# Float32 weights kept in DRAM, low parts moved to VectorE, and steps placed elsewhere in the order of an attention, spectral mixing and FFN kernel

## The chip, the cores and the metric

The kernel runs on one core of a Trainium2 chip. The metric is device time in microseconds; the numbers compared are medians of runs. A core has five engines, each with its own in-order queue: TensorE (PE, with its weight loads as PEld), VectorE (DVE), ScalarE (ACT), GpSimd (POOL) and SyncE (SP), which here issues all transfers between DRAM and the on-chip memory. Matrix products land in PSUM, from which VectorE or ScalarE must take them.

## The reference

```python
# q, k, v: (8, 12, 448, 64); w_ch1: (768, 3072); w_ch2: (3072, 768); float32
scores = scale * np.matmul(q, k.transpose(0, 1, 3, 2)) - np.log(S)
attn = 1.0 / (1.0 + np.exp(-scores))
x = np.matmul(attn, v)             # heads side by side: (8, 448, 768)
mixed = np.real(fft(fft(x, axis=1), axis=2))
u = x + mixed
un = (u - mean(u)) / sqrt(var(u) + 1e-06)
out = u + np.maximum(un @ w_ch1, 0.0) @ w_ch2
```

## The kernel before

The 8 x 448 = 3584 tokens go through three stages.

**Attention and mixing** (the first 445 us or so, with a remainder up to about 485). Scores, sigmoid, values and the two Fourier transforms as products with cosine and sine tables; u is written to DRAM (`u_dram`). The largest weight is looked for here too, because the weights are scaled by a power of two (`wsc`).

**Two plain chunks** of 512 tokens each, numbers c = 0 and 1; the text calls them the first and the second chunk. A loop over f = 0..23 takes one 128-wide slice of the hidden layer at a time. TensorE does `up_proj(c, f)` (18 products into `psh`) and then `down_proj(c, f-1)` (24 products into `po`). `evac(c, f)` lies between: ScalarE writes the high half of the relu'd values, `hh` (float16), and VectorE the low half, `hl` = relu - hh. Each product of float32 numbers is made from three float16 products (high*high, high*low, low*high), and so the weights need high and low parts too.

In the first chunk the weights are made while they are used. There are 48 slices (24 of w1, 24 of w2; the list `order`), about two slots per iteration f, and a slot is `prep_step(k, 0..3)`, which calls `prep_w` for the slice at place k and for its neighbours: step 0 issues the load of slice k+2 and finishes slice k-1 (n == 4), step 1 is ScalarE's absolute value of slice k+1 (L381), steps 2 and 3 are VectorE's four instructions that turn slice k's float64 bits into a float32 number, `t` (tile `wt`; L383, L385, L389, L391). n == 4 scales `t` (L397, ScalarE), writes the high part `h` (L398, ScalarE) and the low part `l` = t - h (L399, GpSimd). An iteration in the engines' queues is: slot A, `evac`, slot B.

In the second chunk the parts are there already. Beside its products, `combine(i, p, n)` makes the sums of weight blocks that the fast chunks need, for 24 pairs of slices: n = 0 rebuilds float32 from h + l (tile `raw`), n = 1 makes four block sums (`cb`), n = 2 their high parts on ScalarE (`ch`), n = 3 their low parts on VectorE (`cl`), n = 4 writes them to `w_dram`. `made_at` says at which f. `fast_norm` (steps placed by `norm_at`) normalises and transposes the tokens of the first fast chunk: load of U, statistics, reciprocal root (`rsqrt`), scaling (L322, VectorE), transposes of 128 x 128 blocks on TensorE (`pst`, L674), copies, differences, and high and low parts (`ut`).

**Five fast chunks** of 512 tokens. Two 2 x 2 block products are each done with seven block products instead of eight (`UP_PRODUCTS`, `DOWN_PRODUCTS`: number of the product, index of the weight block, index of the token or value block). The order is a list of units: `fast_up` (9 products into one PSUM tile `psf`) or `fast_down` (6 products into `pso`), about 1 us each, 28 units per group g (7 up, 7 down, 7 up, 7 down), 6 groups per chunk, so 168 units per chunk. `later(d, fn)` puts a step d units further on in all queues. ScalarE and VectorE take each unit's PSUM tile (8 tiles, `ps_r`); relu, sums and the high and low parts of the hidden values (`F`, `H`) follow over the next units. `fast_norm` of the next chunk's two token halves (tp = 0, 1) is placed by the `later(t + ...)` lines, t being the chunk's first unit. A chunk's last products fall into the first 28 units of the chunk behind it; `fast_finish` then adds up the seven accumulators (`add`, L843), adds the residual (`put`, L847) and writes the output.

After every unit and iteration, `pin()` chains the instructions of each engine in the order in which the code made them, so that each queue runs in the order of the code.

## Time and profile before

| what | value |
|---|---|
| median of 3 runs | 1811.41 us (1811.26 to 1812.59) |
| the profiled execution's own time | 1814.86 us |
| its span, first to last instruction | 1813.1 us |
| PE busy | 1674.0 us (92%) |
| DVE busy | 1332.5 us (73%) |
| ACT busy | 640.3 us (35%) |
| POOL busy | 278.6 us (15%), none of it after about 671 us |
| mean granted TensorE clock | 0.972 |

Busy shares are means over stages with different limits; rows of one stage tell more. A wait is put down to whatever released it last. A granted clock of 1 is 2.4 GHz and of 0.5 is 1.2 GHz. Line numbers are those of the kernel before; the changed kernel's are one to five higher.

### The profile page before, as it was taken

To read this page: it belongs to the slowest core of one execution; us is meant where nothing else is said; L and a number is where in the kernel's file an instruction comes from. 1 tells how busy PE (TensorE), PEld (TensorE's weight loads), DVE (VectorE), ACT (ScalarE), POOL (GpSimd) and SP (SyncE) were. 2 spreads that over 40 slices of the span, in tenths; PEclk is the share of its full clock that TensorE was granted. 3 is DMA by queue.
4 is the path that set the end of the run, shared out by engine and by line. 5 is a ranking of instruction groups with operands and counts; after the bars stand their busy time and mean duration, and the time that the engine had idled before them with its cause. 6 is when DMAs were issued, how large, how long until landed. Compare 5 with 4: busy or idle time off the path is not lost.

```text
span 1813.1 us, 27651 instructions
## 1 busy us (share of the span) xinstructions
PE 1674.0 (92%) x10996; PEld 1070.8 (59%) x10996; DVE 1332.5 (73%) x2481; ACT 640.3 (35%) x815; POOL 278.6 (15%) x268
## 2 busy tenths in 40 slices
PE   8999999988888889897969998999899989999997
PEld 4555555544544445444547775777577757777774
DVE  3445576657999976788756878687868787877667
ACT  4434444435565641222214321422233223323221
POOL 4534444335334430000000000000000000000000
PEclk9999999999999999898989999999899999999999
DMA  7666767664555534444683654656465646565561
GB/s 230 212 211 198 240 206 229 203 194 118 190 162 170 173 124 148 148 168 170 217 312 143 231 221 165 241 220 229 166 231 211 236 177 233 193 233 230 218 229 55
DMA packets 98772, 357.21 MB, mean 197 GB/s; under 512 B 22369, under 2 KB 48210, under 8 KB 83154
## 3 DMA queue, kind: packets, MB, share of 16 engines
q1 hardware_dynamic: 98642, 355.44, 55.7%
q8 instruction: 86, 1.41, 0.3%
q14 instruction: 44, 0.36, 0.1%
HBM read 297.20 MB, written 55.05 MB: 194 GB/s over the span
## 4 chain that ended last, share of the span: by engine, by line
PE 37%; DVE 10%; ACT 2%; issue 1%; ACTq 0%; DVEq 0%
PE psf L769 18%; PE pso L820 18%; DVE F L775 2%; DVE acc L843 2%; DVE H L775 1%; ACT H L804 1%; DVE acc L829 1%; DVE ur L847 1%; PE pst L674 1%; ACT F L794 1%; DVE X L775 1%; DVE stt L295 1%; DVE U L322 0%; DVE mv L316 0%; DVE mv L315 0%
## 5 line engine op out<-in xcount | busy, mean ns | idle before, releaser
L769 PE MATMUL psf<-ut,ws 128*128 128x256 f16 x3780 | 426.7, 273 | 10.9 <-DVE ur L573 9.1
L820 PE MATMUL pso<-ws,H 128*128 128x384 f16 x2520 | 428.1, 329 | 3.3 <-ACT H L804 2.3
L769 PEld LDWEIGHTS <-ws 128*128 128x128 f16 x3780 | 371.0, 98 | 63.0 <-issue 12.4
L820 PEld LDWEIGHTS <-H 128*128 128x128 f16 x2520 | 248.5, 99 | 163.0 <-issue 6.5
L135 ACT ACTIVATE a<-sc 112x900 f32<-112x900 f32 x192 | 166.7, 918 | 163.8 <-PE sc L131 163.8
L829 DVE TENSOR_TENSOR acc<-pso,acc 128x384 f32<-128x384 f32 x350 | 181.2, 550 | 23.3 <-PE pso L820 23.3
L794 ACT ACTIVATE F<-F 128x1024 f32<-128x1024 f32 x60 | 63.5, 1058 | 381.1 <-DVE F L775 374.2
L151 PE MATMUL av<-a,vr 112*64 112x450 f32 x768 | 172.5, 572 | 3.7 <-DVE xT L160 3.7
L775 DVE TENSOR_TENSOR H<-F,H 128x1024 f16<-128x1024 f32 x120 | 129.5, 1088 | 55.8 <-ACT H L804 55.8
L552 PE MATMUL po<-w2h,hl 128*128 128x512 f16 (+1 forms) x384 | 129.0, 336 | 23.1 <-DVE hl L541 22.9
L533 PE MATMUL psh<-ut,w1h 128*128 128x512 f16 x504 | 149.9, 379 | 0.0
L775 DVE TENSOR_TENSOR F<-X,psf 128x256 f32<-128x256 f32 x240 | 98.9, 418 | 69.2 <-PE psf L769 67.1
L552 PE MATMUL po<-w2h,hh 128*128 128x512 f16 (+1 forms) x384 | 129.2, 337 | 8.1 <-ACT hh L540 7.3
L804 ACT ACTIVATE H<-F 128x1792 f16<-128x1792 f32 x60 | 101.8, 1697 | 88.1 <-DVE F L775 86.4
L160 DVE TENSOR_SCALAR xT<-av 128x450 f32<-128x450 f32 x48 | 30.1, 627 | 136.2 <-PE av L151 136.1
L552 PE MATMUL po<-w2l,hh 128*128 128x512 f16 (+1 forms) x384 | 128.9, 336 | 0.0
L552 PEld LDWEIGHTS <-hh 128*128 128x128 f16 x768 | 75.5, 101 | 62.7 <-ACT hh L540 17.2
L775 DVE TENSOR_TENSOR F<-F 128x256 f32<-128x256 f32 x240 | 91.2, 421 | 18.0 <-ACT F L794 13.2
L391 DVE SCALAR_TENSOR_TENSOR wt<-wr,wt 128x768 int32<-128x768 int32 x48 | 100.4, 2091 | 1.7
L151 PEld LDWEIGHTS av<-a,vr 112*64 112x64 f32 x768 | 48.0, 140 | 83.6 <-issue 68.8
L533 PE MATMUL psh<-ut,w1l 128*128 128x512 f16 x252 | 95.5, 379 | 0.0
L775 DVE TENSOR_TENSOR X<-X,psf 128x256 f32<-128x256 f32 x180 | 74.7, 415 | 28.1 <-PE psf L769 23.0
(95 smaller groups left out, 2066.4 us busy)
## 6 DMA issues: line engine op xcount, KB each, us to landing
ws<-w_dram SPq DMA_DIRECT2D x120, 1344.0 KB, 6.0
wr<-w_in SPq DMA_DIRECT2D x96, 768.0 KB, 4.5
qr<-q_in SPq DMA_DIRECT2D x48, 225.0 KB, 3.3
kr<-k_in SPq DMA_DIRECT2D x48, 224.0 KB, 3.5
vr<-v_in SPq DMA_DIRECT2D x24, 448.0 KB, 3.8
w_dram<-ch SPq DMA_DIRECT2D x24, 384.0 KB, 2.3
w_dram<-cl SPq DMA_DIRECT2D x24, 384.0 KB, 2.4
u_dram<-u SPq DMA_DIRECT2D x24, 336.0 KB, 4.1
```

The source lines that it names most:

```text
L135: nc.scalar.activation(a, ps[:CP, :, :SQ], AF.Sigmoid, bias=-math.log(S), scale=1.0 / math.sqrt(D))
L151: nc.tensor.matmul(ps[j * D:(j + 1) * D, :SQ], vr[:, c, h * D:(h + 1) * D], a[:, j], start=(c == 0), stop=(c == 3))
L391: nc.vector.scalar_tensor_tensor(out=ti, in0=hi, scalar=-0x40000000, in1=ti, op0=ALU.bitwise_and, op1=ALU.bitwise_or)
L533: nc.tensor.matmul(hs[c, f], l[f][:, m], r[:, m], start=(m == n == 0), stop=(m == NCC - 1 and n == 2))
L552: nc.tensor.matmul(po[n][:, at:at + hi - lo], l[:, cols], r[f][:, lo:hi], start=(f == 0 and m == 0 and at == 0), stop=(f == NFC - 1 and m ...
L769: nc.tensor.matmul(ps[:, :TH], w[:, x, a, m * 128:(m + 1) * 128], ut[y][:, b, m], start=(m == n == 0), stop=(m == n == 2))
L775: nc.vector.tensor_tensor(out=o, in0=x, in1=y, op=op)
L794: nc.scalar.activation(F[:, 0:4], F[:, 0:4], AF.Relu)
L804: nc.scalar.activation(hts[P][:, 0], F[:, 1:8], AF.Copy)
L820: nc.tensor.matmul(ps[:, :384], H[:, x, a, tp * 128:(tp + 1) * 128], w[:, y, b], start=(j == n == 0), stop=(j == 1 and n == 2))
L829: later(0, lambda: nc.vector.tensor_tensor(out=to, in0=ps[:, :384], in1=to, op=ALU.add))
L843: nc.vector.tensor_tensor(out=a[:, o], in0=a[:, o], in1=a[:, x], op=ALU.add)
```

## The change

- `prep_w`: one ScalarE instruction less per slice: the high part is made straight from `t` with the scale as operand, and now at n == 3, so at the end of the slice's own slot. The unscaled float32 `t` is written to a new DRAM tensor `t_dram` (384 KB per slice). The low part is made on VectorE, as t * scale - h, where n == 4 stood.
- `combine`: n = 0 is now a load from `t_dram` (768 KB), one iteration earlier, in place of two VectorE additions. The four sums are made in place, in other block orders, and scale is applied in n = 2 and n = 3.
- `made_at` and `norm_at`: pairs are spread otherwise over f (two at once at f = 9 and 16 instead of f = 1 and 12), and the transposes stand one f further behind the scaling.
- In the fast chunks `fast_norm` starts at unit 40 instead of 8 for the first half and at 98 instead of 88 for the second, and its transposes stand 8 units behind the scaling instead of 2. Both product tables have other orders, and `fast_finish` is called for every product of the last group, with each sum right behind the product that completes it, instead of all eleven steps behind the seventh.

```diff
@@ -45,8 +45,8 @@
 NPLAIN = 2
 NP = NFC // 2
 
-UP_PRODUCTS = ((1, 1, 1), (6, 4, 4), (7, 5, 5), (5, 3, 3), (2, 2, 2), (4, 0, 6), (3, 6, 0))
-DOWN_PRODUCTS = ((1, 2, 6), (6, 4, 1), (7, 5, 2), (5, 3, 0), (2, 0, 4), (4, 1, 3), (3, 6, 5))
+UP_PRODUCTS = ((1, 1, 1), (6, 5, 4), (7, 3, 5), (5, 4, 3), (2, 2, 2), (4, 0, 6), (3, 6, 0))
+DOWN_PRODUCTS = ((1, 2, 6), (2, 0, 4), (6, 4, 1), (7, 5, 3), (4, 1, 0), (5, 3, 2), (3, 6, 5))
 TH = TW // 2
 
 BANKS = tuple(x for i in (0, 2) for x in (
@@ -69,6 +69,7 @@
         cpool = top.enter_context(tc.tile_pool(name="cpool", bufs=1))
         dram = top.enter_context(tc.tile_pool(name="dram", bufs=1, space=DRAM))
         u_dram = dram.tile([NT, DM], F32, name="u_dram")
+        t_dram = dram.tile([2, NP, 128, 2, DM], F32, name="t_dram")
         w_dram = dram.tile([2, NP, 128, 2, 7, 384], F16, name="w_dram")
         ident = cpool.tile([128, 128], F32, name="ident")
         wmax = cpool.tile([128, 2, NFC], F32, name="wmax")
@@ -390,13 +391,17 @@
                         out=ti, in0=lo, scalar=29, in1=ti, op0=ALU.logical_shift_right, op1=ALU.bitwise_or)
                     nc.vector.scalar_tensor_tensor(
                         out=ti, in0=hi, scalar=-0x40000000, in1=ti, op0=ALU.bitwise_and, op1=ALU.bitwise_or)
-                elif n == 4:
+                if n >= 3:
                     h, l = (x[f] for x in ((w1h, w1l), (w2h, w2l))[i])
                     if i == 0:
                         h, l = (x.rearrange("p c f -> p (c f)") for x in (h, l))
-                    nc.scalar.activation(t, t, AF.Copy, scale=wsc[:, i:i + 1])
-                    nc.scalar.activation(h, t, AF.Copy)
-                    nc.gpsimd.tensor_tensor(out=l, in0=t, in1=h, op=ALU.subtract)
+                    sc = wsc[:, i:i + 1]
+                if n == 3:
+                    nc.scalar.activation(h, t, AF.Copy, scale=sc)
+                    nc.sync.dma_start(t_dram[i, f // 2][:, 1 - f % 2], t)
+                elif n == 4:
+                    nc.vector.scalar_tensor_tensor(
+                        out=l, in0=t, scalar=sc, in1=h, op0=ALU.mult, op1=ALU.subtract)
 
             def prep_step(k, n):
 
@@ -609,37 +614,33 @@
 
             def combine(i, p, n):
 
-                h, l = ([x[f].rearrange("p c f -> p (c f)") if i == 0 else x[f] for f in (2 * p + 1, 2 * p)]
-                        for x in ((w1h, w1l), (w2h, w2l))[i])
                 if n == 0:
-                    made[i, p] = raw = wpre.tile([128, 4, 384], F32, tag="wr", name="raw", bufs=3)
-                    for j in range(2):
-                        nc.vector.tensor_tensor(
-                            out=raw[:, 2 * j:2 * j + 2].rearrange("p s n -> p (s n)"), in0=h[j], in1=l[j], op=ALU.add)
+                    made[i, p] = t = wpre.tile([128, 4, 384], F32, tag="wr", name="cb", bufs=3)
+                    nc.sync.dma_start(t.rearrange("p s n -> p (s n)"), t_dram[i, p].rearrange("p j n -> p (j n)"))
                 elif n == 1:
-                    raw = made[i, p]
-                    made[i, p] = cb = wpre.tile([128, 4, 384], F32, tag="wr", name="cb", bufs=3)
-                    r, t = ([x[:, j] for j in range(4)] for x in (raw, cb))
+                    t = made[i, p]
                     for o, x, y, op in (
-                            ((t[0], r[0], r[1], ALU.add), (t[1], t[0], r[2], ALU.subtract),
-                             (t[2], r[2], r[0], ALU.subtract), (t[3], r[3], t[1], ALU.subtract)),
-                            ((t[0], r[3], r[2], ALU.subtract), (t[1], r[1], t[0], ALU.subtract),
-                             (t[2], r[1], r[3], ALU.subtract), (t[3], r[0], t[1], ALU.subtract)))[i]:
-                        nc.vector.tensor_tensor(out=o, in0=x, in1=y, op=op)
+                            ((1, 0, 1, ALU.add), (0, 2, 0, ALU.subtract),
+                             (2, 1, 2, ALU.subtract), (3, 3, 2, ALU.subtract)),
+                            ((2, 3, 2, ALU.subtract), (3, 1, 3, ALU.subtract),
+                             (1, 1, 2, ALU.subtract), (0, 0, 1, ALU.subtract)))[i]:
+                        nc.vector.tensor_tensor(out=t[:, o], in0=t[:, x], in1=t[:, y], op=op)
                 elif n == 2:
-                    cb = made[i, p]
-                    ch = wpre.tile([128, 4, 384], F16, tag="wt", name="ch", bufs=3)
-                    nc.scalar.activation(ch, cb, AF.Copy)
-                    made[i, p] = cb, ch
+                    t = made[i, p]
+                    h = wpre.tile([128, 4, 384], F16, tag="wt", name="ch", bufs=3)
+                    nc.scalar.activation(h, t, AF.Copy, scale=wsc[:, i:i + 1])
+                    made[i, p] = t, h
                 elif n == 3:
-                    cb, ch = made[i, p]
-                    cl = wpre.tile([128, 4, 384], F16, tag="wt", name="cl", bufs=3)
-                    nc.vector.tensor_tensor(out=cl, in0=cb, in1=ch, op=ALU.subtract)
-                    made[i, p] = ch, cl
+                    t, h = made[i, p]
+                    l = wpre.tile([128, 4, 384], F16, tag="wt", name="cl", bufs=3)
+                    nc.vector.scalar_tensor_tensor(
+                        out=l, in0=t, scalar=wsc[:, i:i + 1], in1=h, op0=ALU.mult, op1=ALU.subtract)
+                    made[i, p] = h, l
                 else:
-                    for j, (x, b) in enumerate(zip(made.pop((i, p)), (h, l))):
+                    for j, (x, b) in enumerate(zip(made.pop((i, p)), ((w1h, w1l), (w2h, w2l))[i])):
                         to = w_dram[i, p][:, j]
-                        b = [y.rearrange("p (s n) -> p s n", s=2) for y in b]
+                        b = [(b[f].rearrange("p c f -> p (c f)") if i == 0 else b[f]).rearrange(
+                            "p (s n) -> p s n", s=2) for f in (2 * p + 1, 2 * p)]
                         if i == 0:
                             nc.sync.dma_start(to[:, 3:7], x)
                             nc.sync.dma_start(to[:, 0:1], b[0][:, 1:2])
@@ -700,15 +701,16 @@
 
             norm_at, made_at = {}, {}
             for j in range(NFC):
-                f = 1 + j * (NFC - 2) // NFC
-                made_at.setdefault(f, []).extend((j, n) for n in range(3))
+                f = 1 + j - (j > 8) - (j > 16)
+                made_at.setdefault(f - 1, []).append((j, 0))
+                made_at.setdefault(f, []).extend((j, n) for n in (1, 2))
                 made_at.setdefault(f + 1, []).extend((j, n) for n in (3, 4))
             for x in made_at.values():
-                x.sort(key=lambda x: (x[1] < 3, x))
+                x.sort(key=lambda x: (x[1] < 3, x[1] > 0, x))
             for tp in range(2):
-                for f, steps in enumerate(((0,), (), (1, 2), (3, 4, 5, 6, 7), (8, 9), (10,), (11,), (12,),
-                                           (13, 14, 15), (16, 17))):
-                    norm_at.setdefault(1 + 10 * tp + f, []).extend((tp, n) for n in steps)
+                for f, steps in enumerate(((0,), (), (1, 2), (3, 4, 5, 6, 7), (8, 9), (), (10,), (11,), (12,),
+                                           (13, 14), (15, 16), (17,))):
+                    norm_at.setdefault(11 * tp + f, []).extend((tp, n) for n in steps)
             prev = None
             for c in range(NPLAIN):
                 for f in range(NFC):
@@ -827,8 +829,8 @@
                     later(0, lambda: nc.scalar.activation(to, ps[:, :384], AF.Copy))
                 else:
                     later(0, lambda: nc.vector.tensor_tensor(out=to, in0=ps[:, :384], in1=to, op=ALU.add))
-                if g % NQ == NQ - 1 and r == 6:
-                    fast_finish(c, tp)
+                if g % NQ == NQ - 1:
+                    fast_finish(c, tp, no)
 
             def fast_residual(c, tp):
                 urs[c, tp] = u = wpre.tile([128, 2, DM], F32, tag="wr", name="ur", bufs=3)
@@ -836,7 +838,8 @@
                     r0 = c * TW + k * TH + tp * 128
                     nc.sync.dma_start(u[:, k], u_dram[r0:r0 + 128, :])
 
-            def fast_finish(c, tp):
+            def fast_finish(c, tp, no):
+
                 a, u = accs[c, tp], urs[c, tp]
 
                 def add(o, x):
@@ -852,10 +855,10 @@
                     elif n == 1:
                         nc.sync.dma_start(out[r0:r0 + 128, :], u[:, k])
 
-                steps = ((add, 2, 1), (put, 2, 0, 0), (add, 6, 1), (add, 7, 6), (add, 3, 5), (add, 3, 6), (put, 3, 0, 1),
-                         (add, 4, 7), (put, 4, 1, 0), (add, 5, 7), (put, 5, 1, 1))
-                for n, x in enumerate(steps):
-                    later(0 if c == NCK - 1 and tp else 1 + n // 2, lambda x=x: x[0](*x[1:]))
+                for x in {2: ((add, 2, 1), (put, 2, 0, 0)), 6: ((add, 6, 1),), 7: ((add, 7, 6),),
+                          4: ((add, 4, 7), (put, 4, 1, 0)), 5: ((add, 7, 5), (add, 6, 5), (put, 7, 1, 1)),
+                          3: ((add, 3, 6), (put, 3, 0, 1))}.get(no, ()):
+                    later(0, lambda x=x: x[0](*x[1:]))
 
             def fast_unit(fn, *args):
                 fn(*args)
@@ -869,7 +872,7 @@
                 t = (c - NPLAIN - 1) * NQ * NU
                 for tp in range(2):
                     for n in range(18):
-                        later(t + 8 + 80 * tp + (8 + 2 * n if n else 0), lambda c=c, tp=tp, n=n: fast_norm(c, tp, n, ps_r))
+                        later(t + 40 + 58 * tp + (10 + 2 * n + 6 * (n > 9) if n else 0), lambda c=c, tp=tp, n=n: fast_norm(c, tp, n, ps_r))
             for g in range(NGR):
                 t = g * NU
                 for d, i, P in ((7, 1, 2 * g), (14, 0, 2 * g + 2), (21, 1, 2 * g + 1), (28, 0, 2 * g + 3)):
```

ScalarE's queue in one iteration of the first chunk. `hh` is the high half of the hidden values, `w1h` and `w2h` are high parts of weight slices, `wt<-wr` is the absolute value of a later slice. Before:

```order
L540 ACTIVATE hh<-psh 128x512
L397 ACTIVATE wt<-wt,wsc 128x768
L398 ACTIVATE w1h_4257<-wt 128x768
L381 ACTIVATE wt<-wr 128x768
L397 ACTIVATE wt<-wt,wsc 128x768
L398 ACTIVATE w2h_4487<-wt 128x768
L381 ACTIVATE wt<-wr 128x768
L540 ACTIVATE hh<-psh 128x512
```

Now:

```order
L545 ACTIVATE hh<-psh 128x512
L382 ACTIVATE wt<-wr 128x768
L400 ACTIVATE w2h_4490<-wt,wsc 128x768
L382 ACTIVATE wt<-wr 128x768
L400 ACTIVATE w1h_4259<-wt,wsc 128x768
L545 ACTIVATE hh<-psh 128x512
```

The high part of slot A's own slice (here `w1h`) now stands directly ahead of `hh`; before, `hh` stood ahead of the instructions for that slice.

VectorE's queue over one iteration of the first chunk, from one `hl` (low half of the hidden values) to the next. Before:

```order
L541 SCALAR_TENSOR_TENSOR hl<-psh,hh 128x512
L383 TENSOR_SCALAR wt<-wt 128x768
L385 TENSOR_SCALAR wt<-wt 128x768
L389 SCALAR_TENSOR_TENSOR wt<-wr,wt 128x768
L391 SCALAR_TENSOR_TENSOR wt<-wr,wt 128x768
L383 TENSOR_SCALAR wt<-wt 128x768
L385 TENSOR_SCALAR wt<-wt 128x768
L389 SCALAR_TENSOR_TENSOR wt<-wr,wt 128x768
L391 SCALAR_TENSOR_TENSOR wt<-wr,wt 128x768
L541 SCALAR_TENSOR_TENSOR hl<-psh,hh 128x512
```

Now:

```order
L546 SCALAR_TENSOR_TENSOR hl<-psh,hh 128x512
L403 SCALAR_TENSOR_TENSOR w1l_4272<-wt,wsc,w1h_4258 128x768
L384 TENSOR_SCALAR wt<-wt 128x768
L386 TENSOR_SCALAR wt<-wt 128x768
L390 SCALAR_TENSOR_TENSOR wt<-wr,wt 128x768
L392 SCALAR_TENSOR_TENSOR wt<-wr,wt 128x768
L403 SCALAR_TENSOR_TENSOR w2l_4511<-wt,wsc,w2h_4490 128x768
L384 TENSOR_SCALAR wt<-wt 128x768
L386 TENSOR_SCALAR wt<-wt 128x768
L390 SCALAR_TENSOR_TENSOR wt<-wr,wt 128x768
L392 SCALAR_TENSOR_TENSOR wt<-wr,wt 128x768
L546 SCALAR_TENSOR_TENSOR hl<-psh,hh 128x512
```

A low part (`w1l`, `w2l`) has come in behind `hl` and behind the other slot's last instruction, each reading a high part that ScalarE makes from the number that VectorE has just finished.

VectorE's queue where the second fast chunk begins, in the units of the second token half's last products and behind them (`acc` and `ur` are accumulators and residual, `X`, `F` the hidden values, `mv` the statistics, `U` the tokens to be scaled). Before:

```order
L847 SCALAR_TENSOR_TENSOR ur<-acc,wsc,ur 128x384
L843 TENSOR_TENSOR acc<-acc 128x384
L775 TENSOR_TENSOR F<-X,psf 128x256
L775 TENSOR_TENSOR X<-X,psf 128x256
L322 TENSOR_SCALAR U<-U,mv 128x768
L847 SCALAR_TENSOR_TENSOR ur<-acc,wsc,ur 128x384
L843 TENSOR_TENSOR acc<-acc 128x384
L775 TENSOR_TENSOR F<-X,psf 128x256
L847 SCALAR_TENSOR_TENSOR ur<-acc,wsc,ur 128x384
L775 TENSOR_TENSOR F<-X,psf 128x256
L322 TENSOR_SCALAR U<-U,mv 128x768
L775 TENSOR_TENSOR F<-X,psf 128x256
```

Now:

```order
L831 TENSOR_TENSOR acc<-pso,acc 128x384
L846 TENSOR_TENSOR acc<-acc 128x384 x2
L850 SCALAR_TENSOR_TENSOR ur<-acc,wsc,ur 128x384
L831 TENSOR_TENSOR acc<-pso,acc 128x384
L846 TENSOR_TENSOR acc<-acc 128x384
L850 SCALAR_TENSOR_TENSOR ur<-acc,wsc,ur 128x384
L777 TENSOR_TENSOR X<-X,psf 128x256 x2
L777 TENSOR_TENSOR F<-X,psf 128x256
L777 TENSOR_TENSOR X<-X,psf 128x256
L777 TENSOR_TENSOR F<-X,psf 128x256 x3
```

The last sums now lie among the products that they add up, and no scaling (L322, now L323) stands in this stretch any more.

## Rows read from the trace of the kernel before

**Rows 1.** Busy time by stretch: length, then PE, PEld, DVE, ACT, POOL, clock, DMA.

```profile
485.70:663.50 177.80, 156.01 (x798) 76.08 (x798) 173.86 (x173) 107.60 (x133) 73.64 (x38) 0.98 0.52 169
683.20:893.50 210.30, 190.29 (x992) 99.52 (x991) 165.25 (x266) 53.40 (x65) 0.00 (x0) 0.94 0.46 166
916.40:1801.40 885.00, 847.42 (x6396) 631.73 (x6395) 679.97 (x1528) 251.04 (x330) 0.00 (x0) 0.98 0.56 209
1801.40:1813.10 11.70, 0.00 (x0) 0.00 (x0) 8.69 (x17) 0.00 (x0) 0.00 (x0) 0.68 0.31 112
```

**Rows 2.** Waits of 485.7 to 663.5: total us, times, longest.

```profile
PE po L552 <- DVE hl L541: 21.4, 18, 1.3
```

**Rows 3.** Timeline of DVE in one iteration there: start, length, instruction.

```profile
560.59 0.68 DVE L541 SCALAR_TENSOR_TENSOR hl<-psh,hh 128x512 f16<-128x512 f32 x1
561.19 0.54 DVE L383 TENSOR_SCALAR wt<-wt 128x768 f32<-128x768 f32 x1
...
563.36 2.28 DVE L391 SCALAR_TENSOR_TENSOR wt<-wr,wt 128x768 int32<-128x768 int32 x1
```

**Rows 4.** Timeline of ACT in the same iteration.

```profile
565.67 0.94 ACT L397 ACTIVATE wt<-wt,wsc 128x768 f32<-128x768 f32 x1 [2.34 <-DVE wt L391]
...
567.39 0.91 ACT L381 ACTIVATE wt<-wr 128x768 f32<-128x768 f32 x1
568.21 0.57 ACT L540 ACTIVATE hh<-psh 128x512 f16<-128x512 f32 x1
```

**Rows 5.** Timeline of POOL in the same iteration.

```profile
562.59 2.23 POOL L399 TENSOR_TENSOR w1l<-wt,w1h 128x768 f16<-128x768 f32 x1 [2.74 <-ACT w1h L398]
```

**Rows 6.** All instructions of line L391: ns min/median/max, first and last start.

```profile
L391 DVE SCALAR_TENSOR_TENSOR wt<-wr,wt x48: 957/2282/2324, 411.7 to 666.2; 128x768 int32<-128x768 int32 x48
```

**Rows 7.** Timeline of PE in the second chunk.

```profile
741.58 1.11 PE L674 MATMUL pst<-ident,U 128*128 128x128 f32 x4 [7.57 <-DVE U L322]
...
781.89 0.59 PE L533 MATMUL psh<-ut,w1h 128*128 128x512 f16 x2
...
789.67 0.59 PE L533 MATMUL psh<-ut,w1h 128*128 128x512 f16 x2
```

**Rows 8.** Groups of DVE in 704 to 893: busy us, mean ns, idle before.

```profile
L617 DVE TENSOR_TENSOR raw<-w1h,w1l 128x768 f32<-128x768 f16 x21 | 19.2, 952 | 0.0
...
L541 DVE SCALAR_TENSOR_TENSOR hl<-psh,hh 128x512 f16<-128x512 f32 x20 | 13.7, 685 | 32.7 <-ACT hh L540 32.7
```

**Rows 9.** Timeline of DVE at the second chunk's end.

```profile
903.53 1.75 DVE L637 TENSOR_TENSOR cl<-cb,ch 128x1536 f16<-128x1536 f32 x1
912.03 3.24 DVE L573 SCALAR_TENSOR_TENSOR ur<-po,wsc,ur 128x512 f32<-128x512 f32 x6 [6.76 <-DMA ur<-u_dram]
```

**Rows 10.** Waits of 904 to 1813.

```profile
PE pst L674 <- DVE U L322: 32.4, 8, 8.6
```

**Rows 11.** Timeline of PE at the start of the second fast chunk.

```profile
1130.08 1.11 PE L674 MATMUL pst<-ident,U 128*128 128x128 f32 x4 [8.62 <-DVE U L322]
1130.98 3.23 PE L820 MATMUL pso<-ws,H 128*128 128x384 f16 x12
1134.05 0.60 PE L674 MATMUL pst<-ident,U 128*128 128x128 f32 x4
1134.49 2.11 PE L820 MATMUL pso<-ws,H 128*128 128x384 f16 x12
```

**Rows 12.** Timeline of PE at the program's end.

```profile
1784.79 16.58 PE L820 MATMUL pso<-ws,H 128*128 128x384 f16 x101
```

**Rows 13.** Timeline of DVE at the program's end.

```profile
1792.63 0.56 DVE L829 TENSOR_TENSOR acc<-pso,acc 128x384 f32<-128x384 f32 x1 [0.42 <-PE pso L820]
...
1809.68 0.62 DVE L847 SCALAR_TENSOR_TENSOR ur<-acc,wsc,ur 128x384 f32<-128x384 f32 x1
```

**Rows 14.** DMA issues by form: count, KB each, median us to landing.

```profile
wr<-w_in SPq DMA_DIRECT2D x96, 768.0 KB, 4.5
w_dram<-ch SPq DMA_DIRECT2D x24, 384.0 KB, 2.3
```

## The prediction

> **What bounds the kernel now.** I read busy time by stretch first, because the change touches four stages with different limits, then the waits and the timeline of each.
>
> In the first chunk VectorE is the bound: 173.9 of 177.8 us busy [rows 1]. Its 173 instructions there are 20 times `hl` and 38 slots of four, so 19 iterations of 177.8 / 19 = 9.36 us. TensorE needs only 7.78 per iteration (the same products one iteration apart in the second chunk, 789.67 - 781.89 [rows 7]) and waits for `hl` [rows 2].
>
> One VectorE instruction there is out of line: L391 takes 2.28, yet at best 0.957 for the same shape [rows 3, 6]. GpSimd's low part runs from 562.59 to 564.82, over the start of L391 at 563.36 [rows 3, 5]. I read this as VectorE held up by GpSimd, 1.33 us per slot.
>
> In the second chunk TensorE is the bound, but 23 iterations of 7.78 are 178.9 and the stretch lasts 210.3 [rows 1, 7]. The excess of 31.4 is waiting for VectorE's scaling (7.57 at 741.58, once more near 838), slow products behind it, and the six transposes themselves (0.44 a piece, 1134.49 - 1134.05 [rows 11], 2.6 in all). VectorE is late because of a loop: `hl` waits 32.7 us in total for `hh` [rows 8], which stands in ScalarE's queue behind the pair's high part, which waits for VectorE's sums.
>
> The fast chunks are bound by TensorE, which loses 32.4 us to transposes that wait for scaled tokens [rows 10]. They stand two units behind the scaling, in the units in which VectorE also does the chunk's last sums. Behind each wait the granted clock is down: four transposes take 1.11 instead of 0.60, twelve products 3.23 instead of 2.11 [rows 11], so 1.6 more.
>
> At the end TensorE is done at 1801.4 and VectorE at 1810.3 [rows 12, 13].
>
> **The change part by part.**
>
> *First chunk, cost.* GpSimd is empty there now, so L391 should take 0.957. But VectorE gets the low part, an instruction of the same size with two inputs from the same memory: 0.96, of which 0.08 overlaps the next as for `hl` (0.68 long, next after 0.60 [rows 3]), so 0.88. By busy time alone an iteration is 0.60 + 2 x (2.17 + 0.957 + 0.88) = 8.61, where 2.17 is from L383's start to L391's [rows 3].
>
> The order says otherwise. Each low part reads a high part that ScalarE can start only when VectorE has finished the number. I follow one iteration. Slot A's four instructions end at 3.13. ScalarE starts 0.03 later (565.67 behind 565.64 [rows 3, 4]) and takes 0.94 (L397 has the same operand scale [rows 4]). `hh` stands behind it now, starts 0.09 before its end (568.21 against 567.39 + 0.91) and takes 0.57 [rows 4]; `hl` starts 0.03 later, at 4.61. VectorE was idle for 1.5. Then `hl` 0.60, low part 0.88: slot B starts at 6.09 and ends at 9.22. Its high part is there at 10.19, the low part starts at 10.22, the next slot at 11.10. So 11.1 us instead of 9.36, 1.74 more, 19 times: **+33**. Three slots ahead of the first `hl` are dearer as well (3.13 + 1.00 + 0.88 = 5.01 against 4.38, half of 9.36 - 0.60): +2. Together **+35**. Bounds: with the high part at 0.84 as L398 is and the low part's step at 0.85, 10.85 and +30; with 0.94 and a step of 1.0, 11.35 and +40. TensorE, at 7.78, hides nothing of it and is hurt by nothing else.
>
> At this place the Trainium skill bears on the change: Perfetto Trace Analysis, "Optimizing Scalar/DVE Operations", says that GpSimd and VectorE share a read port, so that moving work between them might not help. The trace agrees on the sharing (0.957 against 2.28). The same page, "Identifying the Most-Contended Engine", ranks by occupancy; by that the stage would fall to 8.61 per iteration, a gain of 14 us instead of a loss of 35.
>
> The writes to `t_dram` (18.9 MB) go into SP's queue between the loads. Each waits for the L391 for which the next load waits too, so it holds that load only by its issue. It lands in about 2.3 and the load in 4.5 [rows 14]; the next use of either is over 5 us later. I price this at nothing; the cover is half a slot of slack in ScalarE's queue.
>
> *Second chunk, gain.* Per pair two additions of 0.952 [rows 8] go. The loop (`hl` 0.60, low part 1.75 as L637 [rows 9], four sums 2.2, high part 1.5, `hh` 0.5) is then about 6.6, under 7.78, where the additions had made it 8.5. VectorE no longer falls behind, and the transposes stand a further f away. Of 31.4 the transposes' 2.6 stay, and I leave 1.8 for waits of a transpose for the copy ahead of it: **-27**. Bounds: -21 (only the two long waits and the slow products behind them go) and -29. The new load must land within about 7.5 us of its issue, since two iterations are 15.6 and the rest of its loop is 8.1; loads of this size take 4.5.
>
> *Into the fast chunks, gain.* The last low part runs at 903.53 and the residual lands 6.75 behind its end, whereupon eight instructions release TensorE [rows 9]. With VectorE on time the last `up_proj` ends at 893.5 + 4.0, `hl` follows 0.7 and the low part 0.6 later, 898.8: **-4.8**, at least -2.
>
> *Fast chunks, gain.* With 8 units between scaling and transpose, away from the last sums, the 32.4 go, and with them slow products of 1.6 to 2.8 in four places, some 8. At the boundary VectorE has seven accumulations (3.3), sums and low parts of H (3.6) and eleven last sums (6.2) in seven units of 1 us: 6 us behind, while eight PSUM tiles let TensorE run 7 ahead. That leaves next to nothing for PSUM waits, and I count 0.4: **-40**. Bounds: -32 (2 us of such waits at each of four boundaries), and -46 (the slow stretch is worth 3.4 in each place instead of 2).
>
> *End, gain.* The count of last sums is the same; only VectorE's idle 0.4 us per unit in the four or five units ahead of them (one such row [rows 13]) is filled: **-2**, between 0 and -4.5.
>
> Sum: 35 - 27 - 4.8 - 40 - 2 = -39. The profiled execution's span of 1813.1 becomes 1774; it took 1814.9 with what lies around it, 3.4 more than the median of 1811.4. So I forecast 1811.4 - 39 = **1772**.
>
> **The rivals.**
>
> *No stalls in the first chunk.* If the queues overlap more than I think, the occupancy value holds: 49 us less, 1723. Against it: the order has the wait in each slot. 8%.
>
> *The boundary wait moves.* VectorE stays behind by more than 8 units and TensorE waits for PSUM instead; from 9 us on each us costs one per boundary and half. If half of the 40 stays: 1792. For it: VectorE was busy without a break there. Against: thirteen us of norm steps have left. 10%.
>
> *Slower: late loads in the second chunk.* It now writes and loads 2.2 MB per iteration. Should a 768 KB load land 12 us behind its issue, each two iterations take 20.1 instead of 15.6; 11 of them, less 5 us of slack, cost 45, and the total is 1817. It decides from 11.6 us on. Against it: 4.5 now, and TensorE's stage before had a DMA share of 0.46 [rows 1]. 6%.
>
> *The low parts move but L391 stays at 2.28*, if GpSimd is not the cause: 2.65 more per iteration, 50 in all, 1822. The best row of 0.957 speaks against it. 4%.
>
> **How the numbers follow.** 70% for the forecast, whose bounds add up to 30 - 29 - 4.8 - 46 - 4.5 = -54 and 40 - 21 - 2 - 32 = -15, so 1757 to 1796; 8, 10, 6 and 4% for the rivals, 2% for terms that cancel. 1755 to 1797 holds the forecast and the moved wait, 80%. A measurement of this kernel tells 0.2%, 3.6 us, from no change. Faster: 70 + 8 + 10 = 88%; slower 10%; the same 2%.
>
> **What would show it.** In the first chunk: L392 near 0.96, `hl` waiting for `hh` about 1.5 and the low part of w2 for ScalarE about 1.0 per iteration, an iteration of 11.1, GpSimd without work. In the second: iterations of 7.78 and no transpose waiting over 2 us. In the fast chunks: no transposes waiting for L323, at most a us for PSUM per boundary. Wrong would be an iteration of 8.6 in the first chunk (first rival), VectorE waiting for DMA on `cb` (third), or TensorE waiting for `acc` or `ur` (second).

## The result and the profile after

The changed kernel took 1817.05 us (median of 20 executions, 1808.63 to 1824.74), the kernel before 1810.81 (20, 1808.03 to 1813.26) beside it. The ratio is 1.0032, 95% interval 1.0022 to 1.0042: slower by 0.3%, where 1772 (1757 to 1796) and faster was forecast. One execution of a later kernel, `res_early`, took 2482 us at a granted clock of 0.641 and is left out below.

The profiled execution of after was its fastest, 1808.63 us with a span of 1806.8. A second profile of the same code (after_again, below) has a span of 1815.7, nearer to the median, and the sums here go by it where they differ. Line numbers are those of after, and in rows of another run that run's. At the start of the last `psx`, of the second and the twenty-first first-chunk `hl`, of the last `psh` and of the first `psf`, and at the end of the last `pso`, the span divides like this:

| us | before | after | after_again | difference (again - before) | forecast |
|---|---|---|---|---|---|
| start to last `psx` (attention, mixing) | 469.7 | 477.9 | 484.8 | +15.1 | 0 |
| to the second `hl` | 16.0 | 18.7 | 18.7 | +2.7 | +2 |
| to the 21st `hl` (19 iterations) | 177.8 | 213.3 | 213.3 | +35.5 | +33 |
| to the last `psh` (second chunk) | 233.6 | 213.0 | 214.1 | -19.5 | -27 |
| to the first `psf` (switch) | 19.3 | 17.9 | 17.7 | -1.6 | -4.8 |
| to the end of `pso` (fast chunks) | 885.0 | 855.1 | 856.3 | -28.7 | -40 |
| to the end | 11.7 | 10.9 | 10.8 | -0.9 | -2 |

The windows of after, in the columns of [rows 1], for its first three stretches:

```profile
496.60:709.90 213.30, 168.02 (x798) 79.80 (x798) 162.01 (x209) 75.06 (x95) 0.00 (x0) 0.93 0.61 207
729.70:919.20 189.50, 183.96 (x991) 97.59 (x990) 129.67 (x218) 57.47 (x66) 0.00 (x0) 0.99 0.79 276
940.80:1795.90 855.10, 838.94 (x6396) 628.12 (x6395) 684.22 (x1530) 251.38 (x330) 0.00 (x0) 1.00 0.57 217
```

VectorE's work in the first chunk fell from 173.9 to 162.0 us, and yet the stage is 35.5 longer: no engine is full there now. The waits of that stage (total, times, longest) and one iteration on VectorE and on ScalarE:

```profile
ACT w2h L400 <- DVE wt L392: 77.5, 20, 4.0
ACT w1h L400 <- DVE wt L392: 60.0, 18, 3.3
...
PE po L557 <- ACT hh L545: 49.4, 19, 7.8
DVE hl L546 <- ACT hh L545: 28.2, 19, 1.5
DVE w2l L403 <- ACT w2h L400: 19.1, 19, 1.1
```

```profile
590.15 0.96 DVE L392 SCALAR_TENSOR_TENSOR wt<-wr,wt 128x768 int32<-128x768 int32 x1
592.11 1.02 DVE L403 SCALAR_TENSOR_TENSOR w2l<-wt,wsc,w2h 128x768 f16<-128x768 f32 x1 [1.00 <-ACT w2h L400]
...
595.23 0.96 DVE L392 SCALAR_TENSOR_TENSOR wt<-wr,wt 128x768 int32<-128x768 int32 x1
597.67 0.69 DVE L546 SCALAR_TENSOR_TENSOR hl<-psh,hh 128x512 f16<-128x512 f32 x1 [1.49 <-ACT hh L545]
```

```profile
596.22 0.93 ACT L400 ACTIVATE w1h<-wt,wsc 128x768 f16<-128x768 f32 x1 [3.33 <-DVE wt L392]
597.06 0.58 ACT L545 ACTIVATE hh<-psh 128x512 f16<-128x512 f32 x1
```

ScalarE starts the high part at 596.22, when L392 is done; `hh` stands behind it, and `hl` on VectorE behind `hh`. VectorE stands still twice, 1.49 and 1.00. L392 is 0.96, where [rows 3, 6] had 2.28.

The same wait stands where no term was set, in the attention stage. Waits of 395 to 460, then PE's and ACT's timelines at the longest:

```profile
ACT w1p L400 <- DVE wt L392: 24.8, 3, 9.0
...
PE sc L132 <- ACT a L136: 12.8, 3, 6.5
```

```profile
441.97 0.71 PE L132 MATMUL sc<-qh,kh 64*112 64x450 f32 x2 [6.48 <-ACT a L136]
```

```profile
439.31 0.94 ACT L400 ACTIVATE w1p<-wt,wsc 128x768 f16<-128x768 f32 x1 [8.99 <-DVE wt L392]
...
440.91 1.73 ACT L136 ACTIVATE a<-sc 112x900 f32<-112x900 f32 x2
```

Two sigmoids stand behind a high part that waits 8.99 us for VectorE; TensorE needs their PSUM for the next scores. Three slices are prepared in this stage, and three times this happens. In before the scores wait once in this stage, for 4.6:

```profile
PE sc L131 <- ACT a L135: 4.6, 1, 4.6
```

In the fast chunks the wait of [rows 10] is gone, but another is there. PE's waits from 940.8 on (the one for `ur` is the switch), then SP's queue at the first boundary:

```profile
PE psf L771 <- DMA ws<-w_dram: 11.7, 8, 2.3
PE psf L771 <- DVE ur L578: 9.7, 1, 9.7
PE pso L822 <- DVE X L777: 1.8, 4, 0.4
PE pso L822 <- DVE acc L831: 1.6, 2, 0.9
```

```profile
SPq L856 <- DVE ur L850: 33.5, 2, 19.8
```

```profile
1116.77 2.05 SPq L856 DMA_DIRECT2D y_out<-ur  x2
1118.93 0.90 SPq L699 DMA_DIRECT2D ws<-w_dram  x2
1133.55 2.05 SPq L856 DMA_DIRECT2D y_out<-ur  x2
1135.70 0.90 SPq L699 DMA_DIRECT2D ws<-w_dram  x2
```

The change calls the two `put`s that issue a write where their sums are complete, in units 12 and 13 (26 and 27) of a chunk's last group; before, `later(1 + n // 2)` from unit 13 on put them into 17 and 19. The load of the next up-weights stands in unit 14 (28), so the write to `y_out`, at which SP stands up to 19.8 us for VectorE, is now ahead of the load.

### The profile page after: what moved, and what is told of

It reads as the page before. It is cut to its first block, busy times and chain, and to the rows that moved or that the text cites. A ratio compares the mean times of both kernels' runs of the same rounds, so it can differ in the third digit from the quotient of the medians.

```text
span 1806.8 us, 27683 instructions
## 1 busy us (share of the span) xinstructions
PE 1670.1 (92%) x10996; PEld 1069.6 (59%) x10996; DVE 1297.8 (72%) x2481; ACT 603.1 (33%) x767; POOL 193.6 (11%) x220
## 5 line engine op out<-in xcount | busy, mean ns | idle before, releaser
L771 PE MATMUL psf<-ut,ws 128*128 128x256 f16 x3780 | 425.4, 274 | 21.4 <-DMA ws<-w_dram 11.7
L132 PE MATMUL sc<-qh,kh 64*112 64x450 f32 x384 | 82.2, 424 | 18.0 <-ACT a L136 13.4
L546 DVE SCALAR_TENSOR_TENSOR hl<-psh,hh 128x512 f16<-128x512 f32 x48 | 33.1, 690 | 90.5 <-ACT hh L545 90.5
```

The costliest lines, as they stand in the source:

```text
L132: nc.tensor.matmul(ps[:CP, j, :SQ], split[g, 1, kn][h, c * CP:(c + 1) * CP], split[g, 0, qn][h], start=(n == 0), stop=(n == 2))
L771: nc.tensor.matmul(ps[:, :TH], w[:, x, a, m * 128:(m + 1) * 128], ut[y][:, b, m], start=(m == n == 0), stop=(m == n == 2))
```

## The experiments

Times are medians; each ratio is to the kernel before, run beside it on the same chip.

**The two halves apart: order_only and weights_only.** `order_only` is the kernel before with the change's product tables, `norm_at`, places of `fast_norm` and `fast_finish`; `weights_only` is after with these put back:

```diff
-UP_PRODUCTS = ((1, 1, 1), (6, 5, 4), (7, 3, 5), ...
+UP_PRODUCTS = ((1, 1, 1), (6, 4, 4), (7, 5, 5), ...
-                        later(t + 40 + 58 * tp + (10 + 2 * n + 6 * (n > 9) if n else 0), ...
+                        later(t + 8 + 80 * tp + (8 + 2 * n if n else 0), ...
```

In both, the blocks that `combine` makes and the tables that read them no longer belong together, so the fast chunks multiply other blocks; the work is the same.

> The kernel before, with only the later parts of the change: both product tables, the last sums spread over the products, and the tokens' steps moved, in the fast chunks and in the second chunk; weights made as before, without t_dram. Theory (the two halves of the change add up, and the order is worth about 32 us in the fast chunks): 1775 to 1783, no transpose in the fast chunks waiting for scaled tokens. Rival (the fast chunks gained only because the second chunk left VectorE less behind, or the order's gain is given back by loads of w_dram that come late): 1790 to 1811.

> The changed kernel with the tables, the last sums and the tokens' steps put back as before; the weights stay as changed (single scaling by ScalarE, low parts on VectorE, t_dram, pair sums from t_dram in place). Theory: attention's end and the mixing + 16, first chunk + 36, second chunk - 21 or less, so 1835 to 1845. Rival (most of the loss is contention that the new order brings): 1811 to 1825.

Measured: `order_only` 1775.8 us, 0.9803 (0.9778 to 0.9827); `weights_only` 1842.1, 1.0173 (1.0156 to 1.0190), both where the theory had them. By the same marks, attention and mixing take 462.9 in the first and 478.3 in the second, the first chunk 177.8 and 213.3, the fast chunks 852.6 and 883.3: the whole loss is the weights', and nearly all the fast chunks' gain the order's. The second chunk is 229.2 and 212.9, so most of its gain is the weights'; the order alone gives 4.4. `order_only` has the attention of before, and yet 462.9 is 6.8 less than before's 469.7, at a granted clock of 0.99 instead of 0.97 there: a difference between two single profiles is no better than that in this stage. Waits of `order_only` in the fast chunks:

```profile
PE psf L769 <- DMA ws<-w_dram: 9.7, 7, 2.0
```

Loads of `ws` are late here without any `t_dram`: it is not the added traffic.

**The high part one step later, the low part behind it: high_late.**

```diff
-                if n >= 3:
+                if n >= 4:
...
-                if n == 3:
+                if n == 4:
                     nc.scalar.activation(h, t, AF.Copy, scale=sc)
...
-                elif n == 4:
+                elif n == 5:
                     nc.vector.scalar_tensor_tensor(
...
-                for d, m in (((2, 0), (-1, 4)), ((1, 1),), ((0, 2),), ((0, 3),))[n]:
+                for d, m in (((2, 0), (-1, 4)), ((1, 1),), ((0, 2),), ((0, 3), (-1, 5)))[n]:
...
-                for n, d in enumerate((0, 5, 6, 7, 9)):
+                for n, d in enumerate((0, 5, 6, 7, 8, 9)):
```

> The changed kernel with ScalarE's high part one step later (at the start of the next slot, where it stood before the change) and VectorE's low part behind the next slot's number; everything else as changed. Theory (the loss is ScalarE standing still for VectorE with hh and the sigmoids behind it): the first chunk goes to VectorE's busy time, 8.6 us an iteration instead of 11.2, so 50 less, and the waits of the attention's end go, 12 to 16 less: 1745 to 1760. Rival (the low parts cost VectorE so much time, or the t_dram writes so much bandwidth, that the order hardly counts): iteration 10.5 or more, 1795 to 1815.

**The low part back on GpSimd: low_pool.** Scaled `t` goes to `t_dram`; `combine` no longer scales.

```diff
-                if n >= 3:
+                elif n == 4:
...
-                if n == 3:
-                    nc.scalar.activation(h, t, AF.Copy, scale=sc)
+                    nc.scalar.activation(t, t, AF.Copy, scale=wsc[:, i:i + 1])
                     nc.sync.dma_start(t_dram[i, f // 2][:, 1 - f % 2], t)
-                elif n == 4:
-                    nc.vector.scalar_tensor_tensor(
-                        out=l, in0=t, scalar=sc, in1=h, op0=ALU.mult, op1=ALU.subtract)
+                    nc.scalar.activation(h, t, AF.Copy)
+                    nc.gpsimd.tensor_tensor(out=l, in0=t, in1=h, op=ALU.subtract)
```

> The changed kernel with the weights' numbers split as before the change (scaled in place and then rounded by ScalarE, low part on GpSimd), the scaled numbers written to t_dram, and the second chunk's sums taken from t_dram without a further scale. Theory: first chunk at 9.4 an iteration again, attention's end as before, second and fast chunks as changed: 1760 to 1772. Rival (the writes to t_dram are what slows the first chunk and the attention): iteration 10.5 or more, 1790 to 1815.

Measured: `high_late` 1757.1, 0.9696 (0.9673 to 0.9719); `low_pool` 1756.4, 0.9706 (0.9686 to 0.9725), a little under its range. `high_late` does in its first chunk the same VectorE work as after, in 164.1 us instead of 213.3 (8.64 an iteration): the loss was the order, not the work. `low_pool` has 177.7, as before, with the writes to `t_dram` in place, and 464.5 to the last `psx`. VectorE's groups in the first chunk of `low_pool`, then its window and that of `high_late`:

```profile
L392 DVE SCALAR_TENSOR_TENSOR wt<-wr,wt 128x768 int32<-128x768 int32 x39 | 89.2, 2286 | 1.4
L390 DVE SCALAR_TENSOR_TENSOR wt<-wr,wt 128x768 int32<-128x768 int32 x38 | 36.4, 959 | 1.3
```

```profile
480.50:658.20 177.70, 155.98 (x800) 75.53 (x798) 173.76 (x172) 108.15 (x133) 73.65 (x38) 0.99 0.81 251
```

```profile
486.00:650.10 164.10, 152.94 (x799) 76.47 (x798) 159.02 (x210) 78.29 (x96) 0.00 (x0) 0.99 0.91 269
```

With GpSimd at work L392 takes 2286 ns, without it 958 (in after), as I read [rows 3, 5, 6]. In `high_late` VectorE is full again, 159.0 of 164.1.

**Only the attention's slots: att_late.** In these three slots the high part stands one place later (the low part keeps its place); elsewhere all is as in after:

```diff
-                for n, d in enumerate((0, 5, 6, 7, 9)):
+                for n, d in enumerate((0, 5, 6, 7, 8, 9)):
...
-                for d, m in (((2, 0), (-1, 4)), ((1, 1),), ((0, 2),), ((0, 3),))[n]:
+                for d, m in (((2, 0), (-1, 5)), ((1, 1),), ((0, 2),), ((0, 3), (0, 4)))[n]:
```

> The changed kernel, with the high and low parts of the three slots that lie in the attention stage one place later there (the high part behind the next pair's sigmoids); the slots of the mixing and of the first chunk's loop as changed. Theory (three times ScalarE waits 8 to 9 us for VectorE's number with sigmoids queued behind it, which cost TensorE 12.8 us of waiting and 10.2 us at half clock): attention and mixing 372 to 376 instead of 386 to 390, first chunk 213 as changed, median 1801 to 1806. Rival (the attention is longer because VectorE has the low parts there): 384 or more, median 1813 to 1820.

Measured: 1805.8 us (10 executions), 0.9969 (0.9956 to 0.9983), so 11 less than after. The stretch from the first to the last `psx` is 378.3, against 385.6 and 389.5 in the two profiles of after (before: 373.8): a smaller gain than I expected, since ScalarE's sigmoids still hold TensorE for 6.8 us in two places where before has one of 4.6. The place of three instructions in this stage decides whether the kernel is slower or faster than before, by 0.3% either way.

**The loads ahead of the writes: ws_early** (on top of `high_late`).

```diff
-                for d, i, P in ((7, 1, 2 * g), (14, 0, 2 * g + 2), (21, 1, 2 * g + 1), (28, 0, 2 * g + 3)):
+                for d, i, P in ((7, 1, 2 * g), (8, 0, 2 * g + 2), (21, 1, 2 * g + 1), (22, 0, 2 * g + 3)):
```

> The kernel of high_late, with the two loads of up-weights per group issued 6 units earlier, as soon as their buffer is free, so that they stand ahead of the writes of y_out in SP's queue and not behind them. Theory (the waits of psf for ws at a chunk's boundary, 1.0 to 1.8 us twice in each of four boundaries, are SP standing still for VectorE's last sums): none of these waits, fast chunks 10 to 12 less than high_late's 854, and, since fewer waits pull the clock down, a median of 1735 to 1748 with a smaller spread. Rival (the transfers themselves are slow, by bandwidth, or VectorE's last sums hold TensorE through PSUM as soon as the loads don't): fast chunks 848 to 854, median 1752 to 1758.

Measured: 1741.9, 0.9624 (0.9603 to 0.9646). The fast chunks take 846.8 instead of 853.9, not the 10 to 12 less that I expected; PE's waits there show why:

```profile
PE psf L771 <- DVE ur L578: 9.4, 1, 9.4
PE pso L822 <- DVE acc L831: 6.0, 8, 0.9
PE pso L822 <- DVE X L777: 1.8, 4, 0.4
```

No wait for `ws` is left, but 4.6 us came back as waits for a PSUM tile that VectorE has yet to take (6.0 against 1.4 in `high_late`), as the rival has it in its second half. The spread, 1738.7 to 1743.1, is smaller than `high_late`'s 1749.8 to 1759.8, but `mixed` with the same loads has 1730.0 to 1737.1: four executions don't tell.

**Iterations with two pairs: one_pair and stagger.** `one_pair` has `x[:] = [y for y in x if y[0] not in (9, 17) or y[1] == 4]` behind `made_at`, and writes the parts of the pair ahead twice. `stagger` (on top of `res_early`, below) moves only n == 2 of these two pairs to the next f:

```diff
-                made_at.setdefault(f, []).extend((j, n) for n in (1, 2))
+                made_at.setdefault(f, []).append((j, 1))
+                made_at.setdefault(f + (j in (9, 17)), []).append((j, 2))
```

> The kernel of high_late, without load, sums and split of two pairs of the second chunk (the tenth and the eighteenth, those that share an iteration with another); the parts of the pair ahead are written in their place, so two pairs' sums are left out of the computation. Theory (what the second chunk still loses is the two iterations with two pairs, where hh stands behind two high parts): the wait of psh for hl (5.66) and of pst behind it (1.27) go with their 6.8 us at half clock, second chunk 10 less than high_late's 196. Rival (the wait comes from the data traffic of the stage or from the transposes there): 193 to 196.

> The kernel of res_early, with the high part of the tenth and of the eighteenth pair (those that share an iteration with another) one iteration later, behind that iteration's hh. Theory (in these two iterations hh stands behind two high parts, the second of which waits for VectorE's sums): psh's wait for hl of 3.5 us goes, second chunk 4 to 6 less than mixed's 193.4. Rival (the waits come from late loads of cb or from the transposes): 192 or more.

Measured: `one_pair` 1745.8, 0.9649 (0.9616 to 0.9682); its second chunk, by the table's mark, takes 210.0 where `high_late` has 215.7. The wait of `psh` is gone, that of `pst` is still there with 2.2, so 5.7 of the 10 that I expected. The kernel leaves the two pairs out altogether, so 5.7 holds their whole work and not only that they share an iteration. `stagger` 1736.0, 0.9581 (0.9556 to 0.9606): 216.5, no gain on `res_early`'s 215.2 (`psh` still waits 2.8 for `hl`, 5.5 in `res_early`). Its ScalarE waits as long as in `res_early`, where the same high part waits 6.46 for `cb`, but now for a buffer:

```profile
815.76 1.48 ACT L634 ACTIVATE ch<-cb 128x1536 f16<-128x1536 f32 x1 [6.26 <-DMA w_dram<-cl]
817.15 0.58 ACT L678 ACTIVATE U<-pst 128x512 f32<-128x512 f32 x1
817.63 0.59 ACT L548 ACTIVATE hh<-psh 128x512 f16<-128x512 f32 x1
```

`ch` and `cl` share three buffers (`wt`), and one comes free only when its write to `w_dram` has landed. So the two pairs cost what `one_pair` shows, but moving `hh` ahead of the second high part does not win it back. More buffers were not tried.

**GpSimd ahead of the loop, VectorE in it: mixed** (with `ws_early`), **and the residual earlier: res_early** (on top of `mixed`).

```diff
...
+                if n == (4 if k < NPOOL else 5):
+                    e = nc.gpsimd if k < NPOOL else nc.vector
+                    e.tensor_tensor(out=l, in0=t, in1=h, op=ALU.subtract)
...
```

> The loads of ws_early, the numbers scaled in place as before the change with their low parts on GpSimd for the nine slots ahead of the first chunk's loop, and on VectorE, behind the next slot's number, for the other 39. Theory: attention's end as in low_pool (3 to 4 us less than high_late), first chunk 8.64 an iteration as in high_late although ScalarE has two passes again, fast chunks as in ws_early: 1730 to 1745. Rival (ScalarE's second pass makes hh late again): iteration 9.2 or more, 1745 to 1755.

> The kernel of mixed, with the two loads of the second chunk's residual (ur) issued at the start of the last iteration, ahead of the last pair's writes to w_dram in SP's queue and not behind them. Theory (at the switch to the fast chunks TensorE waits 8.6 us for ur, because its load stands behind writes that wait for VectorE's last low parts): that wait falls to 1 to 3 us and its 6.8 us at half clock go or halve, so 16.8 between the last psh and the first psf becomes 8 to 10, the median 1722 to 1727. Rival (the load is late by bandwidth, or its buffer comes free only with the last low part): 1731 to 1735.

Measured: `mixed` 1733.0, 0.9585 (0.9558 to 0.9613), with 464.4 to the last `psx`, 161.3 for the 19 iterations and 845.3 in the fast chunks. It beats before by 4% and after by more. `res_early` 1733.4 (three executions), 0.9568 (0.9547 to 0.9589), in its rival's range: the switch is 12.7 instead of 16.8, of which the second chunk gives back 1.9 (215.2 against 213.3), and the intervals of the two overlap. The wait fell from 8.6 to 4.5, not to 1 to 3: issued at 856.76, the two loads are there at 864.70 and 867.70, when VectorE's instructions on them start. So the two land about 8 and 11 us behind their issue; why so late was not tested.

**The same code again: after_again.**

> The changed kernel once more, for a second profile. Theory (its executions differ by how often the waits at the boundaries of the fast chunks and in the first chunk pull TensorE's clock down): 1813 to 1822, with more than the 86.8 us at half clock of the first profile, the added ones in the fast chunks. Rival (they differ by the length of transfers or by the attention stage): the same time at half clock, other waits longer.

Measured: 1815.2, 1.0023 (1.0007 to 1.0038). The trace's clock records give 98.6 us at half clock, as the theory has it, but the added ones lie ahead of the last `psx` (41.0 instead of 27.3) and not in the fast chunks: there the rival was right. Windows of 0 to 100 and 400 to 450, first profile and second:

```profile
0.00:100.00 100.00, 92.28 (x566) 47.55 (x566) 47.97 (x64) 47.78 (x57) 47.34 (x59) 1.00 0.72 229
...
400.00:450.00 50.00, 37.21 (x194) 20.00 (x196) 35.87 (x58) 21.41 (x29) 20.88 (x17) 0.86 0.41 115
```

```profile
0.00:100.00 100.00, 93.37 (x561) 47.86 (x562) 44.44 (x60) 47.83 (x57) 45.90 (x58) 0.98 0.71 222
...
400.00:450.00 50.00, 35.94 (x176) 20.41 (x178) 36.90 (x58) 18.72 (x26) 25.58 (x22) 0.82 0.41 114
```

Of the 8.9 us between the two spans, 6.9 lie ahead of the last `psx`, and 3.0 of these ahead of the first (92.3 and 95.3; before 95.9). Of all the runs, before, after_again and `att_late` alone have a stretch at half clock near 34 us, and they reach the first `psx` at 95.3 to 95.9, the others at 92.3 to 94.5. So the first profile of after had luck at its start, and so the sums go by the second.

## Why the prediction was wrong, step by step

The seven differences of the table add up to +2.6 in place of -39, while the medians differ by 6.2: the profiled execution of before (1814.86) lies 4.0 over its median, that of after_again (1817.57) 0.5 over that of after. In the prediction's order:

- **First chunk, +33 in the loop: right**, +35.5. The two stalls were forecast at 1.5 and 1.0 and are 1.49 and 1.00; the iteration is 11.23 and not 11.1. `high_late` shows that the cause is the order: with the high part one step later and the low part behind it, the stage comes to 8.64 an iteration, near the 8.61 of the sum by busy time. The Trainium skill (Perfetto Trace Analysis, "Identifying the Most-Contended Engine") ranks engines by occupancy. Its busiest engine gives the length of the stage in `high_late`, and not in after, where no engine is busy for more than 168.0 of 213.3 us.
- **The step that failed first** is "three slots ahead of the first `hl` are dearer as well: +2". That is the remainder only (+2.7). The three slices prepared in the attention stage got no term, though the high part moves there too, in front of sigmoids. The stage got 15.1 longer (15.4 between `order_only` and `weights_only`), the largest single error: TensorE's scores wait 13.1 instead of 4.6 for the sigmoids, and it is at half clock for 41.0 us instead of 23.9. `att_late` takes 11 off the median by moving these high parts alone.
- **Writes to `t_dram` at nothing: right**, by `low_pool`. The cover is thin: in `high_late` ScalarE waits 50.6 us in all for them, without TensorE losing anything that the 8.64 would show.
- **Second chunk, -27: mis-sized**, -19.5. The 23 iterations that the prediction put at 183.3 (178.9, 2.6 and 1.8) took 189.5. The loop of 6.6 us was reckoned for one pair an iteration; two iterations have two, and `one_pair` prices these at 5.7. In after TensorE waits 3.0 for `hl` right behind the second of them, and 2.5 in all for transposes' copies, where 1.8 was left; 3.4 us at half clock follow. The sign that no transpose waits over 2 us was missed, with 2.3. Loads of `cb` held VectorE for 3.9 in all in the first profile of after, so the third rival did not come.
- **Into the fast chunks, -4.8: the step failed**, -1.6. The last low part does start sooner (2.8 behind the last `psh`, 925.69 - 922.89, instead of 903.53 - 897.13 = 6.4), but the residual lands 8.92 behind its end and not 6.76 [rows 9]. `res_early`, a kernel built on `mixed`, shows that part of this is the load's place behind the writes in SP's queue.
- **Fast chunks, -40: mis-sized**, -28.7. The 32.4 went as forecast. The term left out is that the moved last sums issue writes, and that these now pass the loads of the up-weights: 11.7 us of waits. With the loads moved ahead (`ws_early`) the stage is 38.2 under before. PSUM waits, counted as next to nothing, then show up with 6.0.
- **End, -2:** -0.9, within its bounds.

The second rival had the place right (the boundary's wait moves), but the new wait is for a load and not for PSUM. The fourth fell: L392 is 958 ns. The first is what `high_late` makes of the stage, and not after. None of the rivals had the attention. That the measured time lies near the 1817 of the third rival is chance: VectorE waits at most 2.4 us for a `cb`.

What stays open: why `att_late` keeps 378 where `low_pool` has 371. `high_late`, which moves the slots of the mixing too, has 374.5, so perhaps half of it is theirs; but the same code gives 373.8 and 369.2 in the profiles of before and `order_only`, and one profile each doesn't tell.

## What to carry to other kernels

When an instruction moves in a helper, list every call of the helper and, at each, what is queued behind it on that engine; here three calls out of 48 decided the sign. A step that issues a transfer moves in SP's queue too: look for loads behind a write that waits. An instruction that needs another engine's last result belongs a step later, behind work that doesn't.

## What was not expected of the hardware

The time of the same code follows the granted clock: the 20 executions of after run from 1808.63 us at a mean clock of 0.977 to 1824.74 at 0.969, and one profile is not the median. Second, and this was forecast, VectorE's L392 takes 2.4 times as long while GpSimd subtracts beside it (2286 against 958 ns), so that taking over GpSimd's work costs VectorE less (1.01 per slice, L403) than standing beside it (1.33).
